# Talking-heads attention and a squared-ReLU FFN on one core: batch 0's loads, two tilings by a new order, and a check of the row sums

## The chip, the cores and the metric

The kernel runs on one core of one Trainium2 chip. The metric is the device time of one execution in microseconds (us), lower is better. In the profile PE is the matrix engine (PEld its weight loads), DVE, ACT and POOL are the vector, scalar and general engines, SP issues DMAs. "SPq" and "POOLq" are the queues of those engines.

## What is computed

The reference, cut to what matters (B=8 batches, H=12 heads, S=448 positions, D=64; FFN 768 to 2048 to 768 on 3584 tokens):

```python
scores = scale * np.matmul(q, k.transpose(0, 1, 3, 2))
scores = np.einsum('bhij,hg->bgij', scores, w_pre)      # heads are mixed before the softmax
scores = scores - np.max(scores, axis=-1, keepdims=True)
attn = np.exp(scores)
attn = attn / (np.sum(attn, axis=-1, keepdims=True) + 1e-09)
attn = np.einsum('bhij,hg->bgij', attn, w_post)         # and after it
x = np.matmul(attn, v)                                  # laid out as (B*S, 768)
h = np.maximum(x @ w_in, 0.0)
out = h * h @ w_out
```

## The kernel before, in words

All work is written as tasks (`_Task`), each with an engine, its dependencies and a cost in ns that the author gave it. A planner (`_Plan`, L100) fixes the order of every engine's program while the kernel is built. Tasks marked `FLEX` (copies out of PSUM, mostly) may go to ACT or DVE, and the planner picks one. PE's order is given by hand: PE's work stands in ten streams (transposes, scores QK, pre-mixing, post-mixing, AV, "direct" pre-mixing of batch 0, two of the first FFN matmul, two of the second), and the table `ORDER` (L29) is a string of digits, each of which takes the next unit of that stream. Each unit takes one or two of the 8 PSUM banks.

One batch goes through these stages. q and k are loaded as bf16 (`load_qk`, L609), transposed on PE into `qkt` (`emit_T`, L735; the copies out are L460 on ACT and L461 on DVE), and multiplied (`emit_QK`, L908), after which ACT or DVE copy the scores to `stage`. SP's DMAs rearrange `stage` into `dring` (`emit_rel`, L954), so that 10 positions times 12 heads lie on 120 partitions. Pre-mixing (L977) is one matmul with a weight that holds w_pre on blocks. ACT takes the exponential and the row sum in one instruction (L994; no maximum is subtracted), DVE the reciprocal (L1008), POOL multiplies the post-mixing weight with it (L1015), PE mixes (`emit_post`, L1047), and the result is copied to `a2t`. AV (L1104, L1125) gives `xt`. Then the FFN: `emit_F1` (L1173 or L1194), relu on ACT or DVE (L1225, L1226), square on DVE (L1235), `emit_F2` (L1316; its last two tiles L1265), copy to `osb`, and out by POOL's DMA (the last tiles by SP and ACT, L1288).

In batch 0 the first 22 chunks skip the detour over `dring`: `emit_scale` (L834, DVE) multiplies the transposed q by `wq`, which DVE makes from the load `wall` (L547), and `emit_direct` (L856, PE) multiplies that by k and adds over the heads. So the order at the start is: load q and k in three pieces each (pieces 0, 1 and 2, four heads each, called q0, k0 and so on below), transpose, copy out, scale, direct matmuls, exponential.

PE works in four tilings: one tile of 128x128 (full), two tiles of 64 rows (row), two of 64 columns (cols), four of 64x64 (quad). Before, scores in tiles of 128 positions, post-mixing and the FFN from batch 2 on are in row tiling, the FFN of batches 0 and 1 in full, transposes, pre-mixing and the scores of the short tiles in quad, AV in cols. The tiling of a unit is fixed by where it stands in the code:

```python
if b < NFULL:            # emit_F1: batches 0 and 1 in full tiling, one bank each
    ...
    t_h = unit(s_F, "h%d_%d_%d_%d" % (b, c0, t16, x), fn_h, ..., "full", g, NFT)
...
t_h = unit(s_F, "h%d_%d_%d_%d" % (b, c0, t16, ph), fn_h, ..., "row", g, 2 * NFT)
```

In row tiling two units make a pair of 128-wide results in two banks, and the second unit adds to both, so nothing can be copied out before both are done.

Of batch 0's six loads one (q0) goes by SP as float32 into `xt`, and DVE rounds it to `qraw` (`first_q`, L627); the other five go by POOL's queue, which rounds to bf16 on the way (L621).

Of the kernel before, what the change touches and what calls it, by code (L numbers as in the profile page):

```python
# [7 lines left out]
ALU = mybir.AluOpType  # L8
# [21 lines left out]
    "0001155500055555555555555555513155511155555331555533355551135555552005113555555330023324"  # L30
    "2443310041316261116722326772267633227713367333761142441114223667227631167713226671136713"
    "3277620029333912293921812283383338240024442002661118111833381118132672226773136713376224"
    "2444227761136711166333620027622813822383383337771422444200116667733002277622181183118133"
    "8339122922933912291191139333924244422163613731711631622007227363216372227610016733720208"
    "1383338113822291911393119224244422383138311831384222444223621617311716331620027337226336"
    "2127372001636217337220093191119131922833831181138242444222919313933392242444228318331811"
    "1833622267317216362200733733622167200173622367131720029319131931192228181338113822283833"
    "1842244442444238161336220073373362226761171716337610026733724244412812283382020839111911"
    "3913392291192229319138333811382424442283611673317622673137163167122762226733791229339213"
    "98338242444228338338222868633837226773667733677646444876766776678766776879989999899888"  # L40
# [12 lines left out]
class _Task:  # L53
# [3 lines left out]
                 "done", "bias", "sync", "group", "instrs", "issued", "later", "two")  # L57

    def __init__(self, name, engine, fn, deps, after, cost, prio, sem, seminc, mode, dma,
# [21 lines left out]
        self.two = False  # L81
        self.bias = 0.0
# [6 lines left out]
class _Group:  # L89


    __slots__ = ("n", "banks", "readers")

    def __init__(self, n):
        self.n = n
        self.banks = None
        self.readers = [[] for _ in range(n)]


class _Plan:  # L100

    def __init__(self, nbanks):
# [15 lines left out]
        self.warm_up = None  # L118

# [126 lines left out]
    def _commit_pe(self, t, start):  # L246
# [3 lines left out]
        if g is not None and g.banks is None:  # L250
            _, got = self.find(g.n, self.free[PE])
            g.banks = sorted(got)
            for i, readers in zip(g.banks, g.readers):
                for d in self.bank_users[i]:
                    if d not in t.deps:
                        t.deps.append(d)
                self.bank_users[i] = readers
                self.age += 1
                self.bank_age[i] = self.age
        stall, at = self.fetch_wait(t, start)  # L260
        if at is not None:
            self.fetched = at + stall + self.fetch(at + stall)
        held, lat = t.cost[PE]
# [3 lines left out]

    def next_unit(self, order, at):
        if at >= len(order):
            return None  # L270
        t = self.streams[int(order[at])][0]
# [3 lines left out]
        if t.group is not None and t.group.banks is None:  # L275
            est = max(est, self.find(t.group.n, self.free[PE])[0])
# [4 lines left out]
    def run(self, order=""):  # L281
        self.start()
        at = 0
        while True:
# [15 lines left out]
            if f is not None and (best is None or f[0] <= best[0]):  # L300
# [3 lines left out]
                self.streams[int(order[at])].pop(0)  # L304
# [14 lines left out]
def bass_talking_heads_attention__then__ffn_squared_relu_kernel(  # L319
# [44 lines left out]
    with ExitStack() as es:  # L364
# [17 lines left out]
        WC = 256  # L382
        ident = sb("ident", [128, 128], DT.bfloat16)
# [9 lines left out]
        rowsum = sb("rowsum", [128, NPS, 1], DT.float32)  # L393
# [17 lines left out]
        zrow = sb("zrow", [128, S], DT.bfloat16)  # L411

# [10 lines left out]
        sem_hq = Sm("dhq")  # L423
# [7 lines left out]
        sem_last = Sm("olast")  # L431
        sem_out = [Sm("oslot%d" % i) for i in range(NOS)]

        plan = _Plan(NB)

# [13 lines left out]
        def unit(s, name, fn, deps, ns, mode, group, mms):  # L449
# [3 lines left out]
            n = 2 * mms + int(events[kind]) - int(was)  # L453
            t = add(name, PE, fn, deps, c_pe(ns), 0, mode, group, n)
# [85 lines left out]
        t_wall = plan.add("wall", SP, fn_wall, [], {SP: (400.0, 5300.0)}, -1e6 - 1, sem_wq, 16)  # L540
# [68 lines left out]
        def load_qk(b, a, x, u, deps, after, prio):  # L609
            raw, src = ((qraw, q), (kraw, k))[x]  # L610

            def fn(eng, en):
                h = b * H + 4 * a
                if b == 0:
# [896 lines left out]
```

## Time and profile before

| what | value |
|---|---|
| device time, median of 3 runs | 526.7 us (524.83 to 527.67) |
| span of the profiled execution, first to last instruction | 519.0 us |
| what lies around the span (526.7 less 519.0) | 7.7 us |
| PE busy | 505.7 us, 97% of the span, 9632 matmuls |
| ACT / DVE / POOL busy | 418.5 (81%) / 397.4 (77%) / 204.1 us (39%) |
| PE's part of the chain that ended last | 87% |
| moved by DMA | 71.85 MB, mean 138 GB/s |

The page gives no device time for the profiled execution itself, only its span; the sum below is made on the span, and the 7.7 us are added. How to read it: an engine's busy time counts its own instructions; matmuls are pipelined, so a busy PE is only near its peak. The chain that ended last follows each piece of work back to what released it, and its shares say where a microsecond taken away would shorten the run.

### The profile page before, as it was taken

The numbers are of one execution on the slowest core, as the hardware profiler recorded it, in microseconds if no ns is written. First come the engines' busy times: TensorE is split into PE (matmuls) and PEld (weight loads), VectorE is DVE, ScalarE is ACT, GpSimd is POOL, SyncE is SP. The second block draws the span as 40 slices with busy tenths as digits, with TensorE's granted clock in tenths as the row PEclk, the third lists the DMA queues.
The fourth block names the chain that finished last, engine by engine and source line by source line (L and its number), as shares of the span: only waits on it lengthen the run. The fifth ranks groups of instructions, "written<-read, shape, count | busy, mean of one in ns | idle before, by whom it ended". The sixth has DMA issues, their size and how long they took to land.

```text
span 519.0 us, 23210 instructions
## 1 busy us (share of the span) xinstructions
PE 505.7 (97%) x9632; PEld 320.0 (62%) x9632; DVE 397.4 (77%) x999; ACT 418.5 (81%) x1206; POOL 204.1 (39%) x404
## 2 busy tenths in 40 slices
PE   7998999999999999999999999999999999999997
PEld 3455767577776564666555665566556565568874
DVE  6966989889889677978897778975897668865430
ACT  3688999889988889898998889988878886887310
POOL 9913445425651455134632357124722332332000
PEclk9999999999999999999999999999999999999999
DMA  8999999746984689647984679537965557632003
GB/s 156 198 217 170 187 192 194 168 109 146 167 177 106 144 162 183 134 87 164 175 163 91 141 165 182 128 72 156 192 103 111 125 131 139 123 87 66 4 23 99
DMA packets 82560, 71.85 MB, mean 138 GB/s; under 512 B 13434, under 2 KB 79946, under 8 KB 82458
## 3 DMA queue, kind: packets, MB, share of 16 engines
q0 software_dynamic: 36944, 32.81, 38.8%
q1 hardware_dynamic: 45226, 37.38, 30.1%
q8 instruction: 77, 1.26, 1.0%
q10 hardware_dynamic: 288, 0.20, 0.1%
q14 instruction: 25, 0.20, 0.1%
HBM read 45.70 MB, written 11.01 MB: 109 GB/s over the span
## 4 chain that ended last, share of the span: by engine, by line
PE 87%; DMA 5%; DVE 4%; ACT 2%; issue 1%; SPq 1%; POOL 0%; POOLq 0%; DVEq 0%
PE ps L1316 26%; PE ps L1194 18%; PE ps L1047 7%; PE ps L977 7%; PE ps L1173 6%; PE ps L1125 6%; PE ps L908 6%; PE ps L856 5%; DMA dring<-stage 3%; PE ps L1265 2%; DVE stage L461 2%; PE ps L759 1%; DMA qraw<-in_q_dram 1%; PE ps L1104 1%; ACT pring L994 1%
## 5 line engine op out<-in xcount | busy, mean ns | idle before, releaser
L994 ACT ACTIVATE pring<-ps 128x448 bf16<-128x448 f32 x360 | 191.1, 555 | 16.3 <-PE ps L977 10.3
L1316 PE MATMUL ps<-w_out_sb,h2t 64*128 64x384 bf16 x1664 | 152.0, 323 | 0.6 <-issue 0.6
L1015 POOL TENSOR_TENSOR wk2s<-wk2b,rinv 128x120 bf16<-128x120 bf16 (+1 forms) x179 | 69.8, 392 | 189.8 <-DVE rinv L1008 188.6
L461 DVE CAST a2t<-ps 128x480 bf16<-128x480 f32 (+1 forms) x192 | 117.3, 640 | 14.7 <-PE ps L1047 13.2
L1194 PE MATMUL ps<-xt,w_in_sb 64*128 64x448 bf16 (+2 forms) x1344 | 121.9, 323 | 0.2
L461 DVE CAST stage<-ps 128x448 bf16<-128x448 f32 (+1 forms) x174 | 104.5, 617 | 15.4 <-PE ps L908 11.5
L460 ACT ACTIVATE stage<-ps 128x448 bf16<-128x448 f32 (+1 forms) x186 | 96.6, 551 | 23.0 <-PE ps L908 21.1
L1316 PEld LDWEIGHTS ps<-w_out_sb,h2t 64*128 64x128 bf16 x1664 | 77.1, 94 | 52.4 <-issue 3.6
L460 ACT ACTIVATE a2t<-ps 128x480 bf16<-128x480 f32 (+1 forms) x176 | 92.8, 574 | 13.6 <-PE ps L1047 13.2
L1194 PEld LDWEIGHTS ps<-xt,w_in_sb 64*128 64x128 bf16 x1344 | 62.2, 94 | 40.4 <-PE ps L977 2.2
L1348 POOL DMA_DIRECT2D out_dram<-osb x59 | 37.1, 634 | 111.3 <-ACT pring L994 42.2
L994 ACT ACTIVATION_READ_ACCUMULATOR pring<-ps 128x1 f32 x360 | 79.0, 219 | 0.0
L1047 PEld LDWEIGHTS ps<-wk2s,pring 60*128 60x128 bf16 x2880 | 56.1, 93 | 21.4 <-issue 3.1
L1047 PE MATMUL ps<-wk2s,pring 60*128 60x60 bf16 x2880 | 61.1, 187 | 1.0 <-issue 0.3
L1226 DVE TENSOR_SCALAR h1t<-ps 128x448 bf16<-128x448 f32 (+2 forms) x102 | 49.0, 488 | 16.5 <-PE ps L1194 14.1
L1008 DVE RECIPROCAL rinv<-rowsum 128x2 f32<-128x2 f32 (+1 forms) x184 | 29.1, 158 | 35.9 <-ACT pring L994 35.0
L977 PE MATMUL ps<-dring,wk 60*64 60x448 bf16 (+1 forms) x676 | 54.5, 362 | 1.5 <-DVE stage L461 0.6
L1235 DVE TENSOR_TENSOR h2t<-h1t 128x448 bf16<-128x448 bf16 (+2 forms) x176 | 52.6, 332 | 0.5 <-ACT h1t L1225 0.2
L908 PE MATMUL ps<-qkt 64*128 64x448 bf16 (+1 forms) x360 | 49.8, 354 | 1.4 <-issue 1.4
L1225 ACT ACTIVATE h1t<-ps 128x448 bf16<-128x448 f32 (+2 forms) x74 | 32.9, 456 | 19.7 <-PE ps L1194 18.0
L1173 PE MATMUL ps<-xt,w_in_sb 128*128 128x220 bf16 (+1 forms) x384 | 41.7, 260 | 0.1
L1173 PEld LDWEIGHTS ps<-xt,w_in_sb 128*128 128x128 bf16 x384 | 34.6, 98 | 5.7 <-DVE h1t L1226 0.9
(59 smaller groups left out, 419.3 us busy)
## 6 DMA issues: line engine op xcount, KB each, us to landing
dring<-stage SPq DMA_DIRECT2D x309, 105.0 KB
out_dram<-osb POOLq DMA_DIRECT2D x45, 192.0 KB, 4.0
qraw<-in_q_dram POOLq DMA_DIRECT2D x42, 112.0 KB, 5.5
kraw<-in_k_dram POOLq DMA_DIRECT2D x42, 112.0 KB, 5.3
w_in_sb<-in_moe_w_in_dram POOLq DMA_DIRECT2D x8, 384.0 KB, 12.7
w_out_sb<-in_moe_w_out_dram POOLq DMA_DIRECT2D x8, 384.0 KB, 8.7
vraw<-in_v_dram POOLq DMA_DIRECT2D x21, 128.0 KB, 5.1
vraw<-in_v_dram POOLq DMA_DIRECT2D x21, 96.0 KB, 5.3
```

Of the source, the lines that this page charges most:

```text
L460: return eng.activation(o, i_, AF.Copy)
L461: return eng.tensor_copy(o, i_)
L908: r_ = eng.matmul(ps[y * w:(y + 1) * w, g.banks[x], 0:S], qkt[r0:r0 + 64, pb, p + y, 0, i0:i0 + w], qkt[r0:r0 + 64, pb, p + y, 1, :], star ...
L977: r_ = eng.matmul(ps[64 * y:64 * y + 64, gr.banks[x], 0:S], wk1[64 * x:64 * x + 64 - R0 * x, :], dring[64 * x:64 * x + 64 - R0 * x, (g0 + ...
L994: return eng.activation(pring[:, pr, 0:S], ps[:, gr.banks[x], 0:S], AF.Exp, accum_out=rowsum[:, pr, :])
L1015: return eng.tensor_tensor(wk2s[:, p0:p0 + n, :], i0.to_broadcast([128, n, PR]), rinv[:, p0:p0 + n, :].to_broadcast([128, n, PR]), ALU.mult)
L1047: r_ = eng.matmul(ps[:, gr.banks[x], o0:o0 + PR], pring[64 * x:64 * x + PR, pr + y, j0:j0 + 2 * PJ], wk2s[64 * x:64 * x + PR, pr + y, :], ...
L1173: r_ = eng.matmul(ps[:, g.banks[0], 0:n], w_in_sb[:, ft, t * 128:(t + 1) * 128], xt[:, ft, c0:c1], start=(ft == 0), stop=(ft == NFT - 1))
L1194: r_ = eng.matmul(ps[:, g.banks[x], 0:n], w_in_sb[64 * y:64 * y + 64, ft, t * 128:(t + 1) * 128], xt[64 * y:64 * y + 64, ft, c0:c1], start ...
L1226: return eng.tensor_scalar(h1t[:, s, 0:n], ps[:, g.banks[x], 0:n], 0.0, None, op0=ALU.max)
L1235: return eng.tensor_tensor(h2t[:, t16, o0:o0 + n], h1t[:, s, 0:n], h1t[:, s, 0:n], ALU.mult)
L1316: r_ = eng.matmul(ps[:, g.banks[hh], 0:FH], h2t[64 * y:64 * y + 64, t16, col:col + 128], w_out_sb[64 * y:64 * y + 64, t16, hh * FH:(hh + 1 ...
```

## The change

It has five parts.

1. **Loads.** All six q and k pieces of batch 0 are loaded by SP as float32 (`first_load`), into `xt` and the still unused `a2t[1]`, and rounded by a `FLEX` task each, on ACT or DVE. POOL's five loads go; POOL's first load of w_in and its loads of v wait for q1. `wall` stands third in SP's queue.
2. **Two tilings.** A capital letter in `ORDER` takes the next unit of that stream in its other tiling (`choose`): scores in quad (`fn_qk4`), post-mixing in quad (`fn_post4`), a pair of the first or second FFN matmul in full (`fn_hf`, `fn_of`), where each unit of the pair takes its own bank and can be copied out when it is done. `NFULL` goes out of use.
3. **`ORDER`** is another string. Slots of `h1t` are given out in the order in which PE's units are committed.
4. **Row sums.** Each chunk's row sum gets its own column of `rowsum`, 360 in all. After the last exponential DVE takes their maximum and minimum, compares them with two bounds, SP's DMA brings the 128 flags into one row, and DVE reduces them to a verdict.
5. **A second program.** Every engine waits for the verdict, reads it into a register, and jumps over a complete second program (with the maximum subtracted) when it holds. ACT, DVE and SP do so ahead of a tail of their last tasks, PE and POOL at their end.

Core of the diff:

```diff
-    "0001155500055555555555555555513155511155555331555533355551135555552005113555555330023324"
+    "000B010B5550B555555555555555115555555553335555531355555311555553100255311555555330023324"
...
-    "98338242444228338338222868633837226773667733677646444876766776678766776879989999899888"
+    "833384224442288633368382228383722773377363764G444HGGHGIGHHIHGGHGGGHGHIGJHIH8JJJ8999988"
...
+    def choose(self, t, other):
+        if t.alt is None:
+            return
+        if t.group.apart is None:
+            t.group.apart = other
+        if t.group.apart:
+            t.fn, t.cost, t.mode, t.instrs = t.alt
...
-        t = self.streams[int(order[at])][0]
+        s = order[at]
+        t = self.streams[ord(s) - 65 if s.isupper() else int(s, 36)][0]
+        self.choose(t, s.isupper())
...
-        def first_q():
+        def first_load(a, x):
+            n = 2 * a + x
...
             def fn(eng, en):
-                i_ = bass.AP(q.tensor, 0, [[2 * NT * D, 128], [1, 2 * NT * D]])
-                eng.dma_start(part, i_).then_inc(sem_hq.handle, 16)
+                i_ = bass.AP(src.tensor, 4 * a * S * D, [[2 * NT * D, 128], [1, 2 * NT * D]])
+                eng.dma_start(part, i_).then_inc(sem.handle, 16)
...
+            t_c = add("ldqkc_%d_%d" % (a, x), FLEX, fn_cast, [t], ...
...
-                ts.append(load_v(b, u, h0, rows, [last_av.get(b - 1)], after,
+                ts.append(load_v(b, u, h0, rows, [last_av.get(b - 1) if b else first_of[2]], after,
...
-                emit_load_w(0, [], range(1))
+                emit_load_w(0, [first_of[2]], range(1))
...
+                def fn_qk4(eng, en, p=p, g=g):
+                    r_ = None
+                    for x, y in QUADS:
+                        r_ = eng.matmul(
+                            ps[64 * y:64 * y + 64, g.banks[x], 0:S],
+                            qkt[64 * x:64 * x + 64, pb, p, 0, i0 + 64 * y:i0 + 64 * y + 64],
+                            qkt[64 * x:64 * x + 64, pb, p, 1, :],
+                            start=True, stop=True,
+                        )
+                    return r_
...
-                                      accum_out=rowsum[:, pr, :])
+                                      accum_out=rowsum[:, rs, :])
...
+                def fn_hf(eng, en, t=t16 + ph, ph=ph):
+                    r_ = None
+                    for ft in range(NFT):
+                        r_ = eng.matmul(
+                            ps[:, g.banks[ph], 0:n], w_in_sb[:, ft, t * 128:(t + 1) * 128],
+                            xt[:, ft, c0:c1], start=(ft == 0), stop=(ft == NFT - 1))
+                    return r_
...
+        t_v = add("ends", DVE, fn_ends, list(exp_of.values()), {DVE: (1000.0, 1100.0)}, B * 1000.0)
+        t_v = add("low", DVE, fn_low, [t_v], {DVE: (70.0, 160.0)}, B * 1000.0)
+        t_v = add("good", DVE, fn_good, [t_v], {DVE: (70.0, 160.0)}, B * 1000.0)
+        t_v = plan.add("gather", SP, fn_gather, [t_v], {SP: (1000.0, 4000.0)}, B * 1000.0, sem_v1, 16)
+        t_v = add("verdict", DVE, fn_verdict, [t_v], {DVE: (200.0, 300.0)}, B * 1000.0)
...
+        def emit_engine(e, eng):
+            emit(e, eng, [x for x in made[e] if x[0] not in tail])
+            eng.wait_ge(ctr[DVE].handle, verdict_at)
+            ok = eng.value_load(verdict.bitcast(DT.int32))
+            with eng.If(ok == 0):
+                everything(eng, before)
+                emit(e, eng, again[e])
+                everything(eng, after)
+            emit(e, eng, [x for x in made[e] if x[0] in tail])
```

What the planner makes of this is seen in the order of each engine's instructions. In these rows a line number belongs to the file itself: L755 and L830 are batch 0's transposes, L908, L983 and L994 scores (the last in the new quad form), L856 and L931 direct matmuls, L583 and L645 matmuls on a constant that only keep PE running.

PE at the start of the program, before:

```order
L583 MATMUL ps<-warm 128x448 x10
L755 MATMUL ps<-ident,qraw 64x2x32 x28
L583 MATMUL ps<-warm 128x448 x4
L755 MATMUL ps<-ident,kraw 64x2x32 x28
L583 MATMUL ps<-warm 128x448
L755 MATMUL ps<-ident,qraw 64x2x32 x28
L908 MATMUL ps<-qkt 128x448 x4
L856 MATMUL ps<-qkt,w_out_sb 128x448 x6
L755 MATMUL ps<-ident,kraw 64x2x32 x28
L755 MATMUL ps<-ident,qraw 64x2x32 x28
L755 MATMUL ps<-ident,kraw 64x2x32 x28
L856 MATMUL ps<-qkt,w_out_sb 128x448 x39
```

And PE at the same place with the change:

```order
L830 MATMUL ps<-ident,qraw 64x2x32 x28
L994 MATMUL ps<-qkt 64x448 x4
L645 MATMUL ps<-warm 128x448 x2
L830 MATMUL ps<-ident,kraw 64x2x32 x28
L983 MATMUL ps<-qkt 128x448 x2
L830 MATMUL ps<-ident,qraw 64x2x32 x28
L994 MATMUL ps<-qkt 64x448 x4
L931 MATMUL ps<-qkt,w_out_sb 128x448 x6
L830 MATMUL ps<-ident,kraw 64x2x32 x28
L994 MATMUL ps<-qkt 64x448 x4
L931 MATMUL ps<-qkt,w_out_sb 128x448 x30
```

The first row here is q1; four score units instead of two stand ahead of the long row of direct matmuls, and k2's transposes come after the first six direct matmuls instead of the last three pieces together.

DVE in the same stretch, before (L461 copies and rounds, L547 makes `wq`, L834 scales):

```order
L461 CAST qraw<-xt 128x896
L461 COPY qkt<-ps 128x448
L496 TENSOR_TENSOR mask<-mask 128x5
L461 COPY qkt<-ps 128x448
L547 TENSOR_SCALAR wq<-wall 64x180 x4
L834 TENSOR_TENSOR w_out_sb<-qkt,wq 128x8x60 x2
```

DVE there with the change (L523 is the copy, L609 `wq`, L909 scales):

```order
L523 CAST qraw<-xt 128x896
L523 CAST kraw<-a2t1 128x896
L523 COPY qkt<-ps 128x448
L523 CAST qraw<-a2t1 128x896
L609 TENSOR_SCALAR wq<-wall 64x180 x4
L523 COPY qkt<-ps 128x448
L909 TENSOR_TENSOR w_out_sb<-qkt,wq 128x8x60
L523 COPY qkt<-ps 128x448
L523 CAST qraw<-a2t1 128x896
L909 TENSOR_TENSOR w_out_sb<-qkt,wq 128x8x60 x2
L523 CAST kraw<-a2t1 128x896
```

q1's rounding stands ahead of `wq`, those of q2 and k2 among the first scales; k1's goes to ACT, and four of the twelve copies of transposed q and k move from DVE to ACT.

ACT at its end, before (L1225 relu, L1288 the issue of an output DMA):

```order
L1225 ACTIVATE h1t<-ps 128x228 x8
L460 ACTIVATE osb<-ps 128x2x192 x3
L1288 DMA out_0_dram<-osb 64x2x192
L460 ACTIVATE osb<-ps 128x2x192
L1288 DMA out_0_dram<-osb 64x2x192
```

ACT just ahead of the jump with the change (the tail behind it has three copies to `osb` and two DMA issues):

```order
L522 ACTIVATE osb<-ps 128x2x192
L1331 ACTIVATE h1t<-ps 128x228
L522 ACTIVATE osb<-ps 128x2x192 x2
L1644 TENSOR_LOAD warm
L1645 COMPARE_AND_BRANCH
```

The register load and the jump stand between the copies of the FFN's second tile of batch 7 and the tail; on PE they stand behind the last matmul.

More of the change, by code (lines that the diff above doesn't have):

```diff
@@ new lines, in bass_talking_heads_attention__then__ffn_squared_relu_kernel @@
+        users = {}
+        for t in committed:
+            for d in t.deps:
+                users.setdefault(d, []).append(t)
+        tail, closed = set(), {PE, POOL}
+        for t in reversed(committed):
+            e = t.engine
+            if e not in closed and t.end > plan.span - TAIL_NS and all(
+                    u in tail for u in users.get(t, ())):
+                tail.add(t)
+            else:
+                closed.add(e)
+        assert t_v not in tail and all(t in tail for t in odmas if t.sem is sem_last)
```

344 lines of the change are left out of this document (230 added, 114 removed).

## The prediction, made before the changed kernel was run

> **What bounds the kernel now.** I read the page first, then the table of busy time by stage, then the chain of waits and the timeline at the two ends. The page's first lines and its chain:
>
> ```profile
> span 519.0 us, 23210 instructions
> PE 505.7 (97%) x9632; PEld 320.0 (62%) x9632; DVE 397.4 (77%) x999; ACT 418.5 (81%) x1206; POOL 204.1 (39%) x404
> PE 87%; DMA 5%; DVE 4%; ACT 2%; issue 1%; SPq 1%; POOL 0%; POOLq 0%; DVEq 0%
> ```
>
> PE bounds the kernel. The stages show where it stands still (window, length, then busy time of PE, PEld, DVE, ACT, POOL, clock, DMA):
>
> ```profile
> 9.36:43.10 33.74, 33.74 (x462) 17.95 (x464) 26.85 (x80) 25.30 (x71) 18.52 (x33) 1.00 1.19 202
> 43.10:50.50 7.40, 5.35 (x198) 3.70 (x198) 6.20 (x14) 6.74 (x20) 3.01 (x6) 1.00 0.99 172
> 50.50:100.00 49.50, 48.33 (x893) 34.02 (x895) 44.30 (x126) 45.92 (x142) 24.63 (x48) 1.00 0.99 187
> 100.00:200.00 100.00, 99.55 (x2074) 68.82 (x2070) 82.48 (x212) 90.41 (x268) 43.02 (x88) 1.00 0.72 147
> 200.00:300.00 100.00, 98.37 (x1992) 58.57 (x1986) 82.20 (x188) 88.86 (x254) 38.45 (x78) 1.00 0.70 140
> 300.00:400.00 100.00, 99.17 (x2002) 58.65 (x1998) 81.45 (x187) 86.27 (x249) 41.67 (x83) 1.00 0.71 139
> 400.00:515.50 115.50, 115.48 (x1968) 75.53 (x1964) 68.74 (x176) 72.08 (x204) 26.63 (x54) 1.00 0.41 88
> ```
>
> The clock is full throughout. From 9.36 on PE idles 2.05 + 1.17 + 0.45 + 1.63 + 0.83 + 0.02 = 6.15 us. So three things can move the time: the first 9.36 us, these 6.15 us, and how many us the same matmuls take.
>
> **PE's own time.** The change takes no matmul's columns away; it changes tilings. From the chain of waits:
>
> ```profile
> 13.30 7.48 PE ps L856 x39
> 20.78 0.29 PE ps L908 x2
> 21.07 0.23 PE ps L1047 x16
> 21.30 0.19 PE ps L908 x2
> ...
> 56.60 0.50 PE ps L977 x8
> ...
> 57.74 1.80 PE ps L1173 x18
> ```
>
> ```profile
> 485.95 5.83 PE ps L1194 x120
> 491.78 1.30 PE ps L1316 x16
> ...
> 504.98 10.52 PE ps L1265 x64
> ```
>
> The same two score matmuls take 0.29 us behind the full tiling of L856 and 0.19 behind the row tiling of L1047, so a change of tiling costs 0.10. Counted down PE's order, tilings change 244 times before and 254 times after: **+1.0 us**. The other tilings cost nearly the same: L1194 in row takes 5.83/60 = 0.097 per pair of 228 columns, L1173 in full (1.80 - 0.10)/18 = 0.094 per matmul of 220; L1316 1.30/8 = 0.163 per pair, L1265 10.52/64 = 0.164. Fourteen score units go to quad: a quad group of 448 columns (two L977 groups, (0.50 - 0.10)/2) takes 0.20 against 0.19, so +0.2; two post-mixing groups double their matmuls, at most 0.23 each, and I take 0.1 for both, as many small matmuls in four tiles share the time; 0.1 for rounding. Together **+1.4 us**, bounds 1.2 to 1.9.
>
> **The head.** These rows of the timeline (start, duration) and of the DMA view of the first 16 us (GB/s by slices of 0.4 us; issue to landing) carry it:
>
> ```profile
> 0.81 0.40 SPq L632 DMA_DIRECT2D xt<-in_q_dram  x1
> 1.27 0.41 SPq L536 DMA_DIRECT2D wall<-in_w_pre_dram  x1
> 4.06 0.63 DVE L461 CAST qraw<-xt 128x896 bf16<-128x896 f32 x1 [1.15 <-DMA xt<-in_q_dram]
> 7.05 1.20 DVE L547 TENSOR_SCALAR wq<-wall 64x180 bf16<-64x180 f32 x4 [0.60 <-DMA wall<-in_w_pre_dram]
> 8.20 0.63 PE L755 MATMUL ps<-ident,kraw 64*64 64x64 bf16 x28 [1.94 <-DMA kraw<-in_k_dram]
> 9.36 0.63 PE L755 MATMUL ps<-ident,qraw 64*64 64x64 bf16 x28 [0.23 <-DMA qraw<-in_q_dram]
> 10.99 1.53 DVE L834 TENSOR_TENSOR w_out_sb<-qkt,wq 128x480 bf16<-128x480 bf16 x4
> 13.09 1.27 DVE L461 COPY qkt<-ps 128x448 bf16<-128x448 bf16 x4
> ```
>
> ```profile
> GB/s 0 0 0 0 90 99 287 430 269 20 56 38 33 46 123 153 203 206 211 211 215 197 206 215 198 209 210 200 206 200 204 249 187 189 207 205 201 195 198 186
> xt<-in_q_dram SPq DMA_DIRECT2D x1, 448.0 KB, 3.2
> wall<-in_w_pre_dram SPq DMA_DIRECT2D x1, 72.0 KB, 5.8
> ```
>
> SP's queue reached 430 GB/s on q0, 1.07 us for 448 KB. q0 is there at 4.06 as before, k0 then at 5.1, against 8.20. Behind k0 stands `wall`, whose 72 KB went at 20 to 56 GB/s, for about 3.0 us. If the queue runs past it, q1 lands at 6.2, k1 7.3, q2 8.3, k2 9.4; if it holds the queue, each 3.0 later, q1 at 9.2 and k2 at 12.4. `wall` itself, issued 0.4 later and perhaps behind k0, lands at 7.5 to 8.1.
>
> DVE decides what this is worth, since it works in order. From `wq` to the first direct matmul it now does `wq` 1.20, two copies at 1.27/4 = 0.32, three scales at 1.53/4 = 0.38 and q2's rounding 0.63: 3.6 us. `wq` can start at 7.5 to 8.1 (q1's rounding ahead of it ends at 6.8), or at 9.8 if q1 lands at 9.2. The first direct matmul then starts at 11.1 to 11.7 (13.4), and PE needs six of them 1.1, k2's transposes 0.5, scores 0.3 and thirty more 5.7 (7.48/39 = 0.19 each): the 36th ends at 18.7 to 19.3 (21.0). DVE's last scale for them comes 1.20 + 12x0.38 + 6x0.32 + 2x0.63 = 8.9 us after the start of `wq`, 1.5 before it is needed. Before, the 36th ended at 20.78 - 9x0.19 = 19.07, with two score units (0.4) fewer done, so like is 19.47. The head gains 0.8 to 0.2, or loses 1.5. I take **-0.4**, near the rows in which `wall` trickles beside other traffic; bounds -0.8 and +1.5. POOL's w_in and v start 1.2 to 4.2 us later, but five loads of about 1.1 us ahead of them are gone: nothing.
>
> **ACT after the head.** ACT takes one rounding (estimate 0.95, twice the columns of a 0.54 copy), four more copies of q and k, and four score copies that stood among the exponentials before:
>
> ```profile
> 10.32 1.85 ACT L460 ACTIVATE stage<-ps 128x448 bf16<-128x448 f32 x4 [7.04 <-PE ps L908]
> 17.22 0.54 ACT L994 ACTIVATE pring<-ps 128x448 bf16<-128x448 f32 x1 [3.92 <-PE ps L856]
> 44.72 0.68 PE L1047 MATMUL ps<-wk2s,pring 60*128 60x60 bf16 x32 [0.25 <-POOL wk2s L1015]
> 46.51 0.38 PE L1104 MATMUL ps<-a2t,vraw 64*64 64x220 bf16 x8 [0.22 <-ACT a2t L460]
> ```
>
> The 5 us fit into the 11 in which ACT idled, so the stage after 17.22 has 2.2 us less of ACT. What PE waits for at 43 to 47 comes from ACT's exponentials and copies; of the 2.05 us idle there 1.4 are an issue wait (below), so **-0.6**, bounds -0.6 and 0.
>
> **Check and jump.** The row sums have columns of their own and add no instruction. DVE's five small steps fall into the last stage, where DVE is busy 68.74 of 115.5. DVE stands for the gathered flags, a DMA of 2 to 3 us; squares queue behind it, relus on ACT behind those (three slots), PE behind them (eight banks), so PE runs on for some five units of 0.6 us (six L1173 matmuls): 0. If that cover were gone, up to 2. At the end:
>
> ```profile
> 515.52 0.49 ACT L460 ACTIVATE osb<-ps 128x384 f32<-128x384 f32 x1 [5.23 <-PE ps L1265]
> 516.04 0.64 ACTq L1288 DMA_DIRECT2D out_dram<-osb  x1
> out_dram<-osb SPq DMA_DIRECT2D x6, 96.0 KB, 2.2
> q8 instruction: 77, 1.26, 1.0%
> ```
>
> No row shows a register load or a far jump. A block of instructions took 1.0% x 16 x 519 / 77 = 1.1 us to move, a landing 2.2. ACT's jump lies between two copies with 5.23 us of idle time here; PE's lies behind its last matmul at 515.5, beside the last copy, issue and landing, 3.5 us to the span's end. A jump of 3.3 us is just hidden: **0**, bounds 0 and +2.4.
>
> **Sum.** 519.0 + 1.4 - 0.4 - 0.6 + 0 = 519.4; with 7.7 around the span 527.1, against the median 526.7. Other waits of PE I leave as they are, since a new order moves them both ways.
>
> **Rivals.** A measurement of this kernel can tell about 0.5% (2.6 us) from no change, so the same is 524.1 to 529.3.
>
> *The new order removes PE's waits* (faster):
>
> ```profile
> PE ps L908 <- issue: 1.4, 1, 1.4
> PE ps L1125 <- issue: 0.9, 1, 0.9
> ```
>
> These two, in which no engine kept PE waiting, and half of the other 3.8 less the 0.6 counted would give 527.1 - 2.3 - 1.6 = 523.2. For it: a full pair frees its banks one by one, PE has 2% fewer matmuls, and POOL's queue is emptier at 49 and 70 us. Against it: the last stage has only 0.02 us to give and another only 0.45, and ten more changes of tiling are spent.
>
> *DVE stands at the float32 pieces* (slower). `wall` holds SP's queue, q1 lands at 9.2, POOL's w_in starts then; if it takes half of the engines, the last three pieces take 2x1.07 each and k2 lands at 15.6. DVE stands in order at k2's rounding with nine scales behind it; k2's transposes end at 16.8, and scores and thirty direct matmuls 6.0 later, at 22.8: +3.3 instead of -0.4, 530.8. It decides from k2 at about 12.3 on, each us later costs one. For it: 20 to 56 GB/s; against it: POOL's packets began at the same time, and may have been the cause. The Trainium skill ("DMA: Bandwidth & Descriptors", SWDGE vs HWDGE vs iDMA) says that each DMA engine takes turns between the two kinds of queue, which by itself would double the late pieces' time; no row of this trace separates it from `wall`'s own slowness.
>
> *The jump is not hidden* (slower). If PE reads the verdict only when its last matmul is done, a landing 2.2 for the read and 3.3 for the block end at 521.0 against 518.6: 529.5. The Trainium skill ("Runtime: NRT & Kernel Launch", Instruction fetch mechanics) has a taken branch beyond the fetched pages wait for a DMA of the target page, the rule against this change; it gives no length for it, and no row here has such a branch.
>
> **How the numbers follow.** Forecast 527.1 with chance 0.50 (its own range 524.1 to 529.3: the terms at their bounds, without the jump, give 526.5 to 530.1, and the waits left as they are may move it a little either way); waits removed 0.27; DVE at the pieces 0.14; jump 0.09. So faster 0.27, same 0.50, slower 0.23. The range goes from 522.0, past the first rival, to 531.0, past the second.
>
> **What would show it.** Right: PE from about 11 us without a gap, the 36th direct matmul near 19; PE's chain about 1.4 us longer for the same work; the first exponential near 17; 3.5 us from the last matmul to the span's end. Wrong: `wq` starting after 9 us; PE idle in 43 to 515 far from 5.5 us; PE or ACT still at its register load when the last output has landed.

## The result, and the profile after

| | us |
|---|---|
| before, median of 20 runs | 526.35 (521.72 to 533.07) |
| changed, median of 20 runs | 527.61 (524.51 to 534.30) |
| ratio changed / before | 1.0043, 95% interval 1.0023 to 1.0064 |
| forecast | 527.1, range 522.0 to 531.0, chance 0.50 of the same within 0.5% |

The change costs 0.43% (0.0043 x 526.35 = 2.3 us, interval 1.2 to 3.4). That is inside the range and just inside "the same" (0.5%), though its interval reaches beyond. Every ratio in this text compares only executions within 1.5% of the fastest of their kernel, so two of over 1000 us (one of before, one of e2 below) count in none. The forecast's place was right; much of what it was made of was not, and the rest of this text is about that.

First a correction to the base. The profiled execution of the changed kernel took 529.56 us with a span of 527.8, so 1.76 us lie around the span, and the runs of before give 1.8 to 2.0 in the same way. The 7.7 us of the prediction were the distance between a profiled execution of before that was itself a quick one (519.0 + 1.9 = 520.9 us) and the median of others. Hence the two profiled spans, 519.0 and 527.8, must not be subtracted; where a time counts, the ratios do.

The page of the changed kernel, same lines as before:

```profile
span 527.8 us, 22812 instructions
PE 511.4 (97%) x9437; PEld 320.3 (61%) x9437; DVE 392.6 (74%) x982; ACT 431.3 (82%) x1233; POOL 201.4 (38%) x399
PE 87%; ACT 5%; DMA 4%; DVE 2%; issue 1%; POOL 1%; SPq 0%
```

PE still bounds the kernel, with 5.7 us more of busy time. The stages (window, length, then busy time of PE, PEld, DVE, ACT, POOL, clock, DMA):

```profile
9.36:43.10 33.74, 33.34 (x447) 17.24 (x448) 28.25 (x83) 24.41 (x67) 22.12 (x37) 0.91 1.17 201
43.10:50.50 7.40, 7.00 (x158) 3.82 (x158) 4.99 (x12) 6.40 (x19) 2.65 (x5) 1.00 0.83 139
50.50:100.00 49.50, 48.61 (x932) 34.89 (x932) 43.99 (x126) 47.25 (x146) 23.94 (x47) 1.00 1.02 195
100.00:200.00 100.00, 98.52 (x2084) 67.98 (x2081) 83.64 (x209) 91.01 (x266) 43.39 (x87) 1.00 0.71 144
200.00:300.00 100.00, 96.55 (x1874) 56.27 (x1874) 78.83 (x183) 87.35 (x253) 38.72 (x79) 0.98 0.68 139
300.00:400.00 100.00, 97.29 (x1950) 57.09 (x1946) 80.23 (x185) 84.08 (x239) 41.70 (x82) 1.00 0.72 138
```

Two numbers were not there before: the clock is 0.91 in the first stage and 0.98 in the fifth. Inside them it is exactly half:

```profile
8.94:15.76 6.82, 6.00 (x100) 3.39 (x101) 6.20 (x17) 4.70 (x9) 6.40 (x11) 0.50 1.08 242
217.15:220.56 3.41, 3.41 (x59) 1.76 (x59) 1.76 (x3) 1.57 (x4) 0.00 (x0) 0.50 0.50 110
```

The head, from the timeline (start, duration; idle time ahead and what ended it in brackets):

```profile
1.73 0.43 SPq L598 DMA_DIRECT2D wall<-in_w_pre_dram  x1
2.20 0.43 SPq L700 DMA_DIRECT2D a2t<-in_q_dram  x1
6.19 0.63 DVE L523 CAST kraw<-a2t 128x896 bf16<-128x896 f32 x1 [0.94 <-DMA a2t<-in_k_dram]
9.08 0.63 DVE L523 CAST qraw<-a2t 128x896 bf16<-128x896 f32 x1 [1.97 <-DMA a2t<-in_q_dram]
9.62 1.19 DVE L609 TENSOR_SCALAR wq<-wall 64x180 bf16<-64x180 f32 x4
9.76 0.85 PE L830 MATMUL ps<-ident,qraw 64*64 64x64 bf16 x24 [1.78 <-DVE qraw L523]
14.51 1.90 PE L931 MATMUL ps<-qkt,w_out_sb 128*128 128x448 bf16 x6
21.09 0.54 ACT L1082 ACTIVATE pring<-ps 128x448 bf16<-128x448 f32 x1 [2.89 <-PE ps L931]
```

k0 is rounded at 6.19. Then DVE, after one copy, idles 1.97 us until q1 is there at 9.08, and `wq` stands behind q1's rounding: 9.62 against 7.05. PE waits for the same rounding 1.78 us; its transposes then take 0.85 us for 24, at half clock (28 took 0.63), and six direct matmuls 1.90 (1.31). The first exponential comes at 21.09 instead of 17.22, 3.9 us late.

What holds q1 is seen in the DMA view of the first 16 us (slices of 0.4 us; issue to landing):

```profile
GB/s 0 0 0 0 90 143 197 314 314 233 242 278 333 147 89 93 174 275 364 430 421 430 412 403 421 421 383 269 202 164 170 166 156 156 143 159 177 189 197 193
wall<-in_w_pre_dram SPq DMA_DIRECT2D x1, 72.0 KB, 6.2
```

From 5.2 to 6.8 us, while `wall` is moving, the queue falls to 89 to 174 GB/s. POOL's packets start only at 11, so no other queue shares the engines: `wall` is slow by itself, and holds what stands behind it.

### The profile page after: what moved, and what is told of

Read it like the earlier page. It is cut to its first block, busy times and chain, and to the rows that moved or that the text cites. A ratio compares the mean times of both kernels' runs of the same rounds, so it can differ in the third digit from the quotient of the medians.

```text
span 527.8 us, 22812 instructions
## 1 busy us (share of the span) xinstructions
PE 511.4 (97%) x9437; PEld 320.3 (61%) x9437; DVE 392.6 (74%) x982; ACT 431.3 (82%) x1233; POOL 201.4 (38%) x399
## 4 chain that ended last, share of the span: by engine, by line
PE 87%; ACT 5%; DMA 4%; DVE 2%; issue 1%; POOL 1%; SPq 0%
PE ps L1424 24%; PE ps L1289 15%; PE ps L1300 10%; PE ps L1145 8%; PE ps L1064 7%; PE ps L983 5%; PE ps L931 5%; PE ps L1239 5%; DMA kraw<-in_k_dram 2%; ACT pring L1082 2%; PE ps L1372 2%; PE ps L1436 2%; PE ps L834 2%; DMA a2t<-in_q_dram 1%; ACT stage L522 1%
## 5 line engine op out<-in xcount | busy, mean ns | idle before, releaser
L1424 PE MATMUL ps<-w_out_sb,h2t 64*128 64x384 bf16 x1536 | 140.7, 323 | 0.2 <-ACT xt L522 0.2
L523 DVE CAST a2t<-ps 128x480 bf16<-128x480 f32 x195 | 119.4, 638 | 22.9 <-PE ps L1145 21.3
L523 DVE CAST stage<-ps 128x448 bf16<-128x448 f32 (+1 forms) x179 | 107.1, 617 | 12.9 <-PE ps L983 9.5
L1424 PEld LDWEIGHTS ps<-w_out_sb,h2t 64*128 64x128 bf16 x1536 | 70.1, 94 | 47.9 <-issue 3.0
L1289 PE MATMUL ps<-xt,w_in_sb 64*128 64x448 bf16 (+1 forms) x960 | 97.6, 340 | 0.1
L1145 PEld LDWEIGHTS ps<-wk2s,pring 60*128 60x128 bf16 x2848 | 55.9, 94 | 26.4 <-issue 6.2
L1300 PE MATMUL ps<-xt,w_in_sb 128*128 128x228 bf16 (+2 forms) x576 | 67.8, 270 | 0.0
L1145 PE MATMUL ps<-wk2s,pring 60*128 60x60 bf16 x2848 | 62.3, 187 | 4.0 <-issue 3.7
L1289 PEld LDWEIGHTS ps<-xt,w_in_sb 64*128 64x128 bf16 x960 | 43.6, 94 | 35.3 <-issue 1.5
L1300 PEld LDWEIGHTS ps<-xt,w_in_sb 128*128 128x128 bf16 x576 | 52.6, 98 | 12.3 <-ACT pring L1082 1.7
L1064 PE MATMUL ps<-dring,wk 64*64 64x448 bf16 (+1 forms) x676 | 54.7, 363 | 2.9 <-ACT pring L1082 2.5
L1331 ACT ACTIVATE h1t<-ps 128x448 bf16<-128x448 f32 (+2 forms) x96 | 41.3, 443 | 17.5 <-PE ps L1300 9.3
L1332 DVE TENSOR_SCALAR h1t<-ps 128x448 bf16<-128x448 f32 (+2 forms) x80 | 39.9, 507 | 10.8 <-PE ps L1289 7.9
L983 PE MATMUL ps<-qkt 64*128 64x448 bf16 (+1 forms) x332 | 45.7, 354 | 0.0
```

The source lines that it names most:

```text
L523: return eng.tensor_copy(o, i_)
L983: r_ = eng.matmul(ps[y * w:(y + 1) * w, g.banks[x], 0:S], qkt[r0:r0 + 64, pb, p + y, 0, i0:i0 + w], qkt[r0:r0 + 64, pb, p + y, 1, :], star ...
L1064: r_ = eng.matmul(ps[64 * y:64 * y + 64, gr.banks[x], 0:S], wk1[64 * x:64 * x + 64 - R0 * x, :], dring[64 * x:64 * x + 64 - R0 * x, (g0 + ...
L1145: r_ = eng.matmul(ps[:, gr.banks[x], o0:o0 + PR], pring[64 * x:64 * x + PR, pr + y, j0:j0 + 2 * PJ], wk2s[64 * x:64 * x + PR, pr + y, :], ...
L1289: r_ = eng.matmul(ps[:, g.banks[x], 0:n], w_in_sb[64 * y:64 * y + 64, ft, t * 128:(t + 1) * 128], xt[64 * y:64 * y + 64, ft, c0:c1], start ...
L1300: r_ = eng.matmul(ps[:, g.banks[ph], 0:n], w_in_sb[:, ft, t * 128:(t + 1) * 128], xt[:, ft, c0:c1], start=(ft == 0), stop=(ft == NFT - 1))
```

## The experiments

The change and twelve further kernels against before, each on the same chip as its runs of before (95% intervals):

| kernel | loads | order | check | ratio to before |
|---|---|---|---|---|
| the change | new | new | yes | 1.0043 (1.0023 to 1.0064) |
| e7_same, the change again | new | new | yes | 1.0022 (0.9986 to 1.0058) |
| e1_wall_act | new, `wall` by ACT | new | yes | 1.0027 (0.9975 to 1.0080) |
| e5_wall_rows | new, `wall` from 128 rows | new | yes | 1.0039 (1.0008 to 1.0070) |
| e6_wall_pe | new, `wall` by PE | new | yes | 1.0157 (1.0098 to 1.0217) |
| e9_warm_fill | new | new + 9 matmuls | yes | 1.0024 (0.9987 to 1.0060) |
| e12_mixed | half new | new | yes | 1.0022 (0.9982 to 1.0062) |
| e3_old_loads | old | new | yes | 0.9948 (0.9908 to 0.9987) |
| e2_no_check | new | new | no | 0.9975 (0.9937 to 1.0014) |
| e8_order_only | old | new | no | 0.9970 (0.9936 to 1.0003) |
| e4_old_order | new | old | yes | 1.0091 (1.0054 to 1.0128) |
| e10_loads_only | new | old | no | 1.0078 (1.0042 to 1.0114) |
| e11_check_only | old | old | yes | 1.0107 (1.0055 to 1.0159) |

Kernels e1, e2, e5, e7, e9 and the change have the same order on PE, so their exponentials can be compared one by one. End of the n-th exponential in one profiled execution each, us:

| n | e2 | e5 | e9 | e7 | the change | e8 (old loads) |
|---|---|---|---|---|---|---|
| 1st | 19.69 | 18.89 | 20.36 | 21.87 | 21.64 | 18.78 |
| 90th | 124.37 | 124.26 | 124.54 | 126.34 | 125.75 | 124.58 |
| 158th | 213.53 | 212.58 | 213.09 | 212.63 | 212.34 | 211.37 |

The change and e7 are the same kernel. They are 0.3 us apart at the 158th exponential and 4.9 at the 360th and last (484.73 and 479.79), so one execution each shows only roughly where a lead is lost.

### e1_wall_act: `wall` in another queue

```diff
-        t_wall = plan.add("wall", SP, fn_wall, [], {SP: (400.0, 5300.0)}, -1e6 - 1.5, sem_wq, 16)
+        t_wall = plan.add("wall", ACT, fn_wall, [], {ACT: (650.0, 5300.0)}, -1e7, sem_wq, 16)
```

> The changed kernel, with one DMA moved: wall is issued by ACT instead of standing third in SP's queue; the order of PE, DVE, POOL and of all else is the same. Theory A (wall holds SP's queue, and q1's rounding, which stands ahead of wq on DVE, then holds everything): q1 lands near 6.2 us, wq starts near 7.0 instead of 9.6, the first exponential near 18.2 instead of 21.1, and the time is 2.5 to 3.5 us under the changed kernel's, 524.1 to 525.1. Rival B (wall trickles by itself, whatever queue it is in, and wq waits for it): q1 lands near 6.2, but wq still starts after 8.5, and the gain is at most 1 us. Rival C (the head is not what costs): the first exponential moves, and the time stays within 1 us of 527.6.

Neither A nor B came as told. `wall` now runs beside q0, and q0 comes late:

```profile
6.67 0.63 DVE L523 CAST qraw<-xt 128x896 bf16<-128x896 f32 x1 [3.84 <-DMA xt<-in_q_dram]
9.77 1.19 DVE L609 TENSOR_SCALAR wq<-wall 64x180 bf16<-64x180 f32 x4
```

q0 is rounded at 6.67 instead of 4.61, and `wq` starts no earlier. So in this execution `wall` does not only hold its own queue; the transfer beside it is late too. Moving it to another queue moves the damage. The first exponential still starts 1.4 us earlier (19.66 against 21.09), with no half clock after 10.5 us, and the time, 1.0027, is within 1 us of the change, as rival C has it; but the interval (0.9975 to 1.0080) is too wide to see 1.4 us.

### e5_wall_rows: the same 128 descriptors, other addresses

```diff
-            src = bass.AP(w_pre.tensor, 0, [[0, 128], [1, H * H]])
+            src = bass.AP(v.tensor, 0, [[H * H, 128], [1, H * H]])
```

> The changed kernel, but wall's 128 descriptors read 128 different rows of v instead of the same 576 bytes of w_pre (so the pre-mixing weight of batch 0's first 22 chunks is wrong; all counts, sizes and queues are the same). Theory E (the 128 reads of one address wait for each other, some 23 ns each, and hold the pieces behind them): wall's packets are through in under 0.6 us instead of 2.5 to 2.9, q1's rounding starts at 6.3 to 6.8 instead of 9.1, wq near 7, the first exponential at 16.5 to 17.5, and the time is 3 to 4 us under the changed kernel's. Rival F (it is the many small descriptors, or the change of shape in the queue): q1's rounding still starts after 8.5, and the time stays within 1 us.

The same GB/s row, of e5 and then of e7, the change on the same chip:

```profile
GB/s 0 0 0 0 81 116 215 314 341 430 394 345 292 353 360 359 269 385 376 430 421 412 421 394 298 87 135 94 128 162 159 143 110 166 174 187 184 178 164 153
```

```profile
GB/s 0 0 0 0 63 224 269 305 287 367 421 357 52 46 56 36 142 304 329 403 430 412 412 403 394 430 405 266 209 130 155 197 202 195 177 187 195 177 177 188
```

The hole of 36 to 56 GB/s is gone. From the first to the end of the last of `wall`'s 128 packets it takes 1.26 us instead of 3.22. An undisturbed packet takes 27 to 29 ns in both, so what is gone is the time between packets; only the addresses differ, so reads of one address were waiting for each other. Theory E holds for the hole. It does not hold for all of the delay: q1's rounding comes at 8.02, not at 6.3 to 6.8, since q1's own packets take 1.97 us, and why is open. The first exponential starts at 18.35 instead of 21.33. And yet the time is the same: 1.0039 against 1.0022, a difference of 0.17 +- 0.47%, where the 3.0 us would have been -0.57%. The table of exponentials shows where the lead goes: 2.1 us are left at the 90th, none at the 158th.

### e6_wall_pe: one row, spread by a matmul

```diff
-            src = bass.AP(w_pre.tensor, 0, [[0, 128], [1, H * H]])
+            src = bass.AP(w_pre.tensor, 0, [[0, 1], [1, H * H]])
...
+            return eng.matmul(ps[:, g_all.banks[0], 0:H * H], warm[0:1, 0:128], wrow[0:1, :],
+                              start=True, stop=True)
```

> The changed kernel, with one row of w_pre loaded behind q0 (one descriptor of 576 bytes), rounded by DVE to bf16 (1x144), and spread over the 128 partitions by one matmul of PE with a constant column; wq is then made from PSUM. Theory E: q1 lands near 6.3, wq starts at 6.0 to 7.0, the first exponential at 16 to 17, no half clock in the head, and the time is 3 to 4 us under the changed kernel's, 1 to 2 us under the kernel before. Rival C (the head's time is absorbed by later waits): the first exponential moves, the time by less than 1 us.

`wq` starts at 7.74 and the first exponential at 19.25, but the kernel is 1.6% slower (six runs, 529.84 to 541.83). The order of ACT and DVE differs only in the first 32 us. In its profiled execution it is ahead of e7 by 2.1 us at the first exponential and 1.9 at the 69th, then falls back and is 15 us behind at the 293rd, with waits like this one:

```profile
PE ps L996 <- ACT pring L1095: 3.2, 1, 3.2
```

Why is not known. It says nothing on what a lead in the head is worth; as a version it is of no use.

### e7_same and e9_warm_fill: the clock in the head

e7 is the changed kernel again. In e9 the constant matmuls ahead of q1's transposes grow from 2 to 11:

```diff
+            m = n + 9 if sum(t.name.startswith("warm") for t in plan.tasks) == 3 else n
...
-                for _ in range(n):
+                for _ in range(m):
```

> The changed kernel once more, unchanged, as the measure for the others on this chip: 527 to 528, with PE's clock at half for at least one stretch of 3.4 us between 7 and 16 us if the half clock follows PE's idle time there.

> The changed kernel with nine more matmuls on a constant where PE waits for q1's rounding (7.4 to 10 us); the order of all else is the same. Theory G (PE's idle time of 1.6 us and more there brings the half clock): no stretch of half clock between 8 and 16 us, PE's transposes of q1 at 0.56 us instead of 0.85, the first exponential near 19.2 instead of 21.1 to 21.3, and some runs with a mean clock over 0.998, which 0 of 32 runs of the changed kernel had. On the time there are two cases. If the head's time reaches the end: 1.5 to 2 us under the changed kernel. Rival C (the lead is used up by PE's waits up to 160 us): within 1 us of it, and the exponentials from the 157th on at the same time as in the changed kernel.

The stretch of half clock in e7, and the same window in e9 (clock is the number behind the counts):

```profile
9.02:15.85 6.83, 5.72 (x99) 3.24 (x100) 5.92 (x16) 4.53 (x9) 6.12 (x10) 0.50 1.08 248
```

```profile
9.02:15.85 6.83, 5.49 (x138) 2.96 (x137) 6.27 (x17) 4.43 (x9) 6.08 (x10) 1.00 1.04 230
```

PE gets through 138 matmuls there instead of 99. In all 32 timed runs of the change and e7 the mean granted clock was at most 0.997, which is one stretch of 3.4 us at half; 4 of 12 runs of e9 and 45 of 92 of before had 0.999 or more. So theory G holds: PE's wait for q1 brings the half clock, and matmuls on a constant keep it away. The first exponential gains 1.5 us. Whether the time follows is not shown: 1.0024 against 1.0022, but each to within 0.36%, and 1.5 us are 0.29%. The 158th exponential ends 0.5 us later than in e7, which looks like rival C. But in e9's execution the lead is still 1.9 us at the 115th and is lost to a single wait of 1.56 us marked issue (to 156.23) and a stretch of half clock behind it (156.9 to 160.3); e7 has neither, and nothing shows that the fill in the head brings them.

### e2_no_check and the end of the span

The verdict's tasks and this are taken out:

```diff
-            eng.wait_ge(ctr[DVE].handle, verdict_at)
-            ok = eng.value_load(verdict.bitcast(DT.int32))
-            with eng.If(ok == 0):
-                everything(eng, before)
-                emit(e, eng, again[e])
-                everything(eng, after)
```

> The changed kernel without the check of the row sums, the verdict, the jumps and the second program (these parts are left out). Theory A (check and jump lie beside other work): the same time as the changed kernel within 1 us, and 3.5 us from the last matmul to the span's end. Rival D (the jump, or the larger program, costs): 2 to 4 us less, with the gain at the end of the span or in fewer waits marked issue.

The ratio is 0.9975, 0.5 to 0.7% under the two runs of the full change: rival D, if weakly. Where the time goes is seen behind the last output's issue. The DMA view from there to the span's end, of e7 (4.8 us, slices of 0.12) and of e2 (3.1 us, slices of 0.08):

```profile
GB/s 19 0 0 0 0 0 0 0 0 0 0 232 198 198 186 269 333 218 32 6 0 0 0 0 6 13 6 6 13 13 26 19 0 0 0 0 0 0 0 0
q8 instruction: 1, 0.02, 2.0%
out_dram<-osb ACTq DMA_DIRECT2D x1, 96.0 KB, 4.2
```

```profile
GB/s 0 0 0 0 0 0 0 0 0 0 0 0 0 0 0 0 0 69 149 208 248 188 198 208 387 347 357 149 30 0 0 0 0 0 0 0 0 0 0 0
out_dram<-osb ACTq DMA_DIRECT2D x1, 96.0 KB, 2.5
```

In e7 most of the output is out after 2.4 us, in e2 all of it after 2.3. Then, in e7, nothing moves for half a us, and the last packets trickle at 6 to 26 GB/s until 3.8. The one packet of the instruction queue is a page of 16 KB that took 1.55 us (2.0% x 16 x 4.8); it started at 521.21, and the output's last packet ended 0.88 us after the page did. In e3, e5 and e11 the last packet ends the same 0.88 us after such a page, in e1, e4, e9 and e12 0.62 to 0.90. So behind PE's jump a second page is fetched, presumably on a DMA engine that still has its share of the output queued; the kept traces do not name a packet's engine. From the last matmul to the span's end it is 4.9 to 5.7 us in e1, e3, e4, e5, e7, e9, e11 and e12, and 3.5 in the four kernels without the check (before, e2, e8, e10). The profiled execution of the change (3.5) and e6 (3.6) escaped: there the page began when the output was all or nearly through.

### e3_old_loads, e8_order_only, e4_old_order, e10_loads_only, e11_check_only: the parts apart

e3 puts the loads of before back, e8 takes the check out of e3. e4 puts the old string `ORDER` into the change, e10 takes the check out of that, e11 has the old loads and the old string:

```diff
-                        if b == 0:
+                        if (b, a, x) == (0, 0, 0):
                             ts.append(first_load(a, x))
                             continue
```

```diff
-        self.choose(t, s.isupper())
+        self.choose(t, s.isupper() or t.name[:3] in ("h0_", "h1_"))
```

> The changed kernel with the loads of before: q0 and wall by SP, the other five pieces by POOL, which rounds on the way; w_in and v wait for nothing; order, tilings and check stay as changed. Theory A (the head costs 3 to 3.5 us, the new order gives some of it back): wq starts near 7, the first exponential near 17.5, and the time is 2.5 to 3.5 us under the changed kernel's, so 524.1 to 525.1, which is 1 to 2 us under the kernel before. Rival C (the order's extra changes of tiling and waits cost, the head nothing): the time stays at 527 to 528.

> The changed kernel with the loads of before and without the check, the jumps and the second program: what is left of the change is the order and the tilings. Theory A (check and jump are hidden): the same within 1 us as the kernel with the old loads and the check, 524 to 525. Rival D (check and jump cost 2 to 3 us): 521 to 522.

> The changed kernel with the order of before (and so the tilings of before; FFN of batches 0 and 1 in full), loads and check as changed. Theory A (the head costs 3 to 3.5 us, the new order gives back about 2): slower than the changed kernel by 1.5 to 2.5 us, 529 to 530. Rival C (the order costs, the head nothing): 525.5 to 526.5, under the changed kernel.

> The loads of the change alone: order and tilings of before, no check, no jumps, no second program. From the runs so far the loads are worth +2 to +3 us and the check about +1: 527.5 to 529, against 526 of the kernel before. If the 4.8 us of the kernel with loads and check are the loads alone: 530 to 531.

> The check, the jumps and the second program alone: loads, order and tilings of before. Theory A (hidden): 525 to 526.5, as the kernel before. Rival D: 528 to 530, with the time at the end of the span or in more waits for instructions.

With the new order there are all four cells (the change and e7 weighted together: 1.0038). New loads cost 0.05% without the check and 0.90% with it, mean 0.47 +- 0.33% or 2.5 us; the check gives 0.22% with the old loads and costs 0.63% with the new, mean 0.20 +- 0.33% or 1.1 us. The check's price differs in sign between the two pairs; why is open. e3 is 0.9948, the one interval of thirteen that is wholly under 1: the version that beats both kernels is the change with the loads of before, though the best of thirteen looks better than it is.

With the old string all three cells are 0.8 to 1.1% over before, whichever part is in. That fits neither theory: loads and check together (0.91%) cost no more than either alone. What the three share is the changed planner under the old string; e10 waits for transfers where before had 0.3 us of such waits, e11 for slots of `h1t`:

```profile
PE ps L1064 <- DMA dring<-stage: 3.8, 2, 2.4
```

```profile
PE ps L1068 <- ACT h1t L1335: 1.9, 1, 1.9
```

The old string in the changed planner with the old loads and no check was not run, so this stays open; e4, e10 and e11 say nothing on loads or check alone.

e8 shows what the order does by itself, in an execution at full clock as that of before:

```profile
span 520.0 us, 22796 instructions
PE 508.5 (98%) x9438; PEld 319.5 (61%) x9438; DVE 390.5 (75%) x978; ACT 427.6 (82%) x1227; POOL 203.7 (39%) x404
```

PE is busy 2.8 us longer (508.5 against 505.7) and idle 1.8 less (11.5 against 13.3). But much of both lies in the head, where matmuls on a constant run while PE waits. From q1's transposes to the last matmul it is, before and then in e8:

```profile
9.36:515.50 506.14, 499.99 (x9561) 317.24 (x9561) 392.22 (x979) 415.57 (x1202) 195.94 (x386) 1.00 0.70 139
```

```profile
9.16:516.50 507.34, 501.48 (x9367) 316.26 (x9367) 385.50 (x958) 424.67 (x1223) 195.80 (x386) 1.00 0.70 139
```

So there PE is busy 1.5 us longer, of which two more matmuls on the constant are about 0.4, and idle 0.3 less (5.86 against 6.15).

### e12_mixed: q0, k0 and `wall` by SP, the rest by POOL

```diff
-                        if (b, a, x) == (0, 0, 0):
+                        if b == 0 and a == 0:
```

(The minus is e3's line.)

> The changed kernel with q0 and k0 by SP as float32 and wall behind them, and the other four pieces by POOL, which rounds on the way; w_in and v wait for nothing. Theory E (the 128 reads of wall hold what stands behind them in their queue, and here nothing of batch 0 does): wq starts at 7.5 to 8, the first exponential at 17 to 18.5, no half clock in the head; the time as with the loads of before or up to 1 us under it, 523.5 to 525. Rival (wall beside POOL's pieces slows these): q1 after 9.5, 526 and more.

q1's transposes start at 7.97 instead of 9.76, but `wq` only at 8.57: now DVE waits for `wall` itself. The first exponential ends at 19.98, no half clock in the head, 1.0022. No gain on e3.

## Why the prediction held, point by point

- **The head: -0.4, bounds -0.8 and +1.5.** The step that failed is the choice between "the queue runs past `wall`" and "holds": it held (e5 shows the hole and its cause), `wq` started at 9.62 as the upper bound had it (9.8). The bound itself was too low. The 36 direct matmuls end where this row does,

```profile
17.10 5.85 PE L931 MATMUL ps<-qkt,w_out_sb 128*128 128x448 bf16 x30
```

  at 22.95, against 19.47 like for like: +3.5. Of the 2.0 beyond the bound 1.5 are the half clock (e9), which had no place in the sum, because before's trace had none.
- **The head's price at the end.** The prediction passed every us of the head on to the span. e5 shows that it is not so: its lead of 3.0 us at the first exponential is gone by the 158th, and its time is not under e7's. In the executions compared the lead goes into waits that e7 has shorter or not at all: e5 has 2.1 us of waits marked issue for L834 and 1.2 for `stage` between 20 and 190 us, e7 1.1 and none. e9's 1.5 us and e1's 1.4 are too little for the ratios to show. The loads as a whole still cost 2.5 +- 1.8 us on the mean of two pairs, 0.3 and 4.7; which of these is right is not settled.
- **PE tilings +1.4, bounds 1.2 to 1.9.** About right: from q1's transposes on, e8 has 1.5 us more of busy time, or 1.1 without the two further matmuls on the constant. (Fourteen score units at 0.01 each are 0.1 rather than 0.2, which changes nothing.)
- **Waits of PE, left as they are.** The order alone measures -0.30% (-0.64 to +0.03), -1.6 us, not clear of nothing. The traces do not show where a gain would come from: behind the head the waits fall by 0.3 us between the two profiled executions, and that of before was a quick one. So the rival "the new order removes PE's waits" has at most a part of its 527.1 - 523.2 = 3.9.
- **ACT's relief -0.6.** In e8 PE idles 1.29 us at 43.1 to 50.5, of them 1.06 on instructions; before 2.05, of them 1.59. So 0.2 of 0.6.
- **Check and jump 0, bounds 0 and +2.4.** PE's jump is hidden as forecast. In the changed kernel it reads its register 3.1 us before its last matmul ends, and the branch takes 3.9 us (duration in ns):

```profile
L1644 PEldq TENSOR_LOAD <-warm x1: 713/713/713, 521.2 to 521.2; - x1
L1645 PEldq COMPARE_BRANCH  x1: 3897/3897/3897, 522.0 to 522.0; - x1
```

  What failed is the cover: it was counted in time on PE, while the pages of the jump share the DMA engines with the very output that covers it. That lengthens the end of the span by 1.4 to 2.2 us in 8 of the 10 profiled kernels with the check; the ratios, at 1.1 +- 1.8 us, neither confirm nor exclude it. The rival "the jump is not hidden" had the place and nearly the price, with another mechanism. (Its 518.6 stands in no row; from the span's end, 519.0, its price is 2.0, not 2.4.)
- **Sum.** Loads +2.5, check +1.1, order -1.6, each to within 1.8, make +2.0 us against +2.3 measured; forecast +0.4. They come from the four cells and must add up to the 1.0038 of the change and e7, so the sum is no proof of its parts. On these values the errors on head and check were of one sign and that on the waits of the other. That it stayed "the same" then rests on this cancelling, which is luck, and 0.43% is near the edge. Of the signs that were to show it wrong two came: `wq` after 9 us, and PE idle 0.40 + 0.89 + 1.48 + 3.45 + 2.71 = 8.9 us from 43 to 400 instead of 5.5 (with the half clock and two waits of about 2 us in it).

The prediction's rival on DVE had k2's landing and w_in on the same engines as its mechanism. That hardly happened: all but the last 32 of k2's 128 packets had started when POOL's first did, at 11.06. So this case does not test the rule of the Trainium skill that the prediction names there, of engines that take turns between the two kinds of queue. That rival's 36th direct matmul, at 22.8, was near the measured 22.95 by luck, since the wait was at q1; its time, 530.8, was not.

## What to carry to other kernels

A small load that reads one address into 128 partitions can be worse than a load six times its size: put it behind everything that is awaited, or read it once. Ask of each new wait in front of PE whether it is long enough to halve the clock, and fill it if so (here that moved the first exponential, and a gain in time was not shown); but price a gain at the start of a long kernel only after finding the next wait that would use it up. And a jump hidden behind another engine's work is not hidden from the DMA engines: placing it so that its pages land before the last output is issued should avoid that, which no run here tried.

## What the runs showed of the hardware

- 128 reads of the same 576 bytes took 2.5 to 3.2 us from first to last packet in the kernels with the new loads (on average one in 20 to 25 ns), 2.8 to 3.4 beside POOL's packets and 4.1 in e1; 128 different rows took 1.26.
- PE's clock fell to half for 3.41 us or twice that, after PE idle times of 1.8 to 2.7 us (waiting for q1 in the change and e7, and 1.95 at 215), and in e9 of 1.56. e2's 1.55 us brought none, and some of 2 us and more brought none either. The stretches of 3.41 us lie on a grid, and PE's idle time within one of them tells more than the length of a single wait: over the 14 profiled executions, from the first record of the clock on, it was 1.5 to 2.6 us in each of the 13 stretches that ended in a fall, and at most 1.9 in all others. The change's wait of 2.48 us at 379 brought no fall; it lay across two stretches, with 1.7 us idle in the larger part. The Trainium skill ("TensorE: Matmul & The Clock Gate", What's actually happening) has a free-running window of about 3.4 us; the lengths agree. It gives an idle window as what brings the half clock; here one idle for about half of its time was enough, and the exact condition is not shown.
- The waits marked issue look like waits for instructions: in the change the four longest ended 1.2 to 1.5 us after a 16 KB packet of the instruction queue did, and one of 1.95 us was itself followed by half clock:

```profile
217.03 0.71 PE L1145 MATMUL ps<-wk2s,pring 60*128 60x60 bf16 x23 [1.95 <-issue]
```

  The Trainium skill ("Runtime: NRT & Kernel Launch", Instruction fetch mechanics) calls crossing such a page mostly hidden. In this trace 3.7 us at L1145 and 0.9 at L834 were not:

```profile
PE ps L1145 <- issue: 3.7, 3, 1.9
PE ps L834 <- issue: 0.9, 1, 0.9
```

- PE's far jump took 3.4 to 3.9 us, a register load from SBUF 0.48 to 0.72.
